# Sign of float64 weights taken by a parametric ReLU, another order of the first steps, reloads in place

## The chip, the cores and the metric

One core of one Trainium2 chip. The time is the device time of one execution in microseconds, as the median of the runs. TensorE, VectorE, ScalarE and GpSimd run in order, each on its own list; all DMAs are issued from SP's one queue.

## What is computed

Batch 4, 8 heads, 576 positions, 64 columns a head. Attention has two parts: one over q, k and v averaged in groups of 4 positions, repeated 4 times, and one over the neighbours at a distance under 4. Their sum, as 2304 rows of 512, goes through two MLPs of the same form. The weights reach the kernel as float64 words.

```python
def _moe_ref(x, w_in, w_out):
    h = x @ w_in                  # 2304 x 512 by 512 x 2048
    r = np.maximum(h, 0.0)
    g = r * r
    return (g @ w_out).astype(np.float32)

def reference(**kwargs):
    ...
    attn_out = _attn_ref(**attn_kwargs)     # out_up + out_local
    x = np.ascontiguousarray(attn_out.transpose(0, 2, 1, 3)).reshape(B * S, H * D)
    x = _moe_ref(x=x, **moe_kwargs)
    return _moe2_ref(x=x, **moe2_kwargs)
```

## The kernel before

The 2304 rows are 9 tiles of 256, the hidden width 8 blocks `p` of 256. One step (n, p) takes tile n through block p: `mm_h` (line 883) makes h from x and w_in in 24 matmuls, ScalarE makes relu and square in PSUM (lines 895, 897), and `mm_y` (line 967) adds its product with w_out, 24 matmuls in the first layer. Every operand is split in a high and a low float32r half, so that three products stand for one of full float32. The second layer, tiles n = 9 to 17, makes y by seven products of halves (`mm_y2`, line 950, 21 matmuls), for which `quarters` prepares sums of blocks of w_out.

The weights of the first layer are converted at the start by `convert1(p, kind)`, kind 0 for w_in and 1 for w_out: the float64 block is loaded into `s`; ScalarE reads the high words as float32 and scales them into a buffer `g` (line 693), and scales the low words in place (line 695); VectorE puts the sign bit of the high word into the low word's place (line 697), shifts `g` left by 3 and joins it with the low word (line 702); ScalarE copies the result to the high half (line 390 of the helper `evac`), VectorE or GpSimd subtracts for the low half (line 713). `convert2` does the same for the second layer in halves of 512 columns (lines 739, 741, 743, 747) while the first layer runs, and stores the words in DRAM; `reload` (lines 823 to 829) brings them back when the first layer is done with a block: a load into a staging buffer `ld`, a copy to the high half, a subtraction for the low half.

The attention of batch b feeds the tiles: `load_qk` (transposes, line 450, evacuation, line 390, pooling on VectorE, line 457), `pool_v`, `heads_of` (the pooled part), `values`, `group` (the local part; line 619 scales the softmax, line 623 transposes it, line 653 adds both parts to `xr`). `split_x` splits x.

The order of all engines' instructions is written out by a planner when the program is built: the class `Order` holds threads (generators) in lanes of a given width, each with a due time in tiles; it always takes the operation that can start first by its own cost figures, and at a tie the thread of the earliest due time. Conversions are due at `CP + CD * p`, loads of q and k at `t + QP`, the pooling of v at `t + VP`, the heads at `t + HP`, groups and values at their place plus `GP` and `UP`, with t = b * 576 / 256 - 2. What the planner sets is an order for each engine; on the chip an instruction waits for its operands by semaphores, and all that stands behind it on its engine waits too. Until the first step, `fill` puts dummy matmuls between the attention's (line 1121).

The first two tiles go side by side. With `LEAD = 2`, the steps by tile are 0 0 0 1 0 1 0 1 0 1 0 1 0 1 1 1; tile 1's y has a PSUM pair of its own. PSUM pairs `at0`, `at1` and `y` serve the attention until the steps take them.

Of the kernel before, what the change touches and what calls it, by code (L numbers as in the profile page):

```python
# [8 lines left out]
F32 = mybir.dt.float32  # L9
# [5 lines left out]
AF = mybir.ActivationFunctionType  # L15
# [19 lines left out]
NXR = 2  # L35
NVW, NPB, NHD = 2, 2, 2
AHEAD = 4
LEAD = 2
XO = 'PVHL'
XN = [2, 2, 2, 5]  # L40
PO = 80
# [3 lines left out]
FT = 3  # L45
KICK = {(n, 1) for n in (10, 12, 14)}
CL, GL, HL = 4, 4, 6
CP, CD, GP, UP = -0.47, 0.09, -1.99, -1.02
QP, VP, HP = -0.59, 0.34, -0.14


class Thread:
# [162 lines left out]
def attention_two_mlp_kernel(  # L215
# [154 lines left out]
    def dvp(cols):  # L370

        return "DVP", 0.065 + cols / 957.0
# [7 lines left out]
    def act(cols):  # L380
        return "ACT", 0.065 + cols / 1150.0
# [7 lines left out]
    def evac(dst, src):  # L389
        nc.scalar.activation(out=dst, in_=src, func=AF.Copy)  # L390

    def dma(nbytes, run=4096):

        return "SP", nbytes / (16e3 * run) * {256: 22.5, 1024: 88.0, 2048: 142.0, 4096: 212.0}[run]
# [271 lines left out]
    def convert1(p, kind):  # L666
        yield lambda: 0.0
        for slots, i in spare.get((p, kind), []):
            yield from slots.give_up([i])
        st = early[p, kind] if (p, kind) in early else buffer(p, kind, I64, "s")  # L670
        st = st[:, 0:1024]
        if kind == 0:
            t = st.rearrange("p (r i f) -> p r i f", r=2, i=2)
            wv = w_in1.rearrange("(s i r d) f -> s r d i f", s=2, i=2, r=2)
            for r in range(2):
                for s_ in range(2):
                    tt = yield dma(64 * 4096, 2048)
                    nc.sync.dma_start(out=t[64 * s_:64 * s_ + 64, r ^ s_], in_=wv[s_, r][:, :, p * 256:p * 256 + 256])
        else:
            for half in range(2):  # L680
                r0 = p * 256 + half * 128
                tt = yield dma(64 * 8192)
                nc.sync.dma_start(out=st[:, 512 * half:512 * half + 512], in_=w_out1[r0:r0 + 128])
        wf = st.bitcast(F32).rearrange("p (c w) -> p c w", w=2)[:, :, 1]
        wl = st.bitcast(U32).rearrange("p (c w) -> p c w", w=2)[:, :, 0]
        w32 = st.bitcast(I32).rearrange("p (c w) -> p c w", w=2)
        m = yield from f_ga.take()
        parts = [(gp, 0, 1024)] if m == 0 else [(gb[i], 512 * i, 512) for i in range(2)]


        for g, c, n in parts:
            yield act(n)
            nc.scalar.activation(out=g, in_=wf[:, c:c + n], func=AF.Copy, scale=2.0 ** -112)
        yield act(1024)
        nc.scalar.activation(out=wl, in_=wl, func=AF.Copy, scale=2.0 ** -29 - 2.0 ** -49, bias=-0.5)
        yield dvp(1024)
        nc.vector.scalar_tensor_tensor(
            out=w32[:, :, 0], in0=w32[:, :, 1], scalar=-2 ** 31, in1=w32[:, :, 0], op0=ALU.bitwise_and, op1=ALU.bitwise_or
        )
        for g, c, n in parts:  # L700
            yield dvp(n)
            nc.vector.scalar_tensor_tensor(
                out=g.bitcast(I32), in0=g.bitcast(I32), scalar=3, in1=w32[:, c:c + n, 0],
                op0=ALU.logical_shift_left, op1=ALU.bitwise_or,
            )
        hi = weight(p, kind, 0).rearrange("p k f -> p (k f)")
        for g, c, n in parts:
            yield act(n)
            evac(hi[:, c:c + n], g)
        for g, c, n in parts:  # L710
            for lo, c1, n1 in pieces(p, kind, 1, 1, c, n):
                tt = yield either(n1)
                engine().tensor_tensor(
                    out=lo, in0=g[:, c1 - c:c1 - c + n1], in1=hi[:, c1:c1 + n1].bitcast(F32), op=ALU.subtract
                )
        f_ga.put(m, tt)
        count(("w", 1, p), 2, tt)
        count(("w", 1), 2 * NP, tt)

    def convert2(p, kind, half):  # L720
        yield o.at("w", 1)
        n = yield from f_ld.take()
        if kind == 0:
            t = ld[n].rearrange("p (k f) -> p k f", k=2)
            yield dma(64 * 8192, 2048)
            nc.sync.dma_start(
                out=t, in_=w_in2.rearrange("(k p) f -> p k f", p=128)[:, 2 * half:2 * half + 2, p * 256:p * 256 + 256]
            )
        else:
            r0 = p * 256 + half * 128  # L730
            yield dma(64 * 8192)
            nc.sync.dma_start(out=ld[n], in_=w_out2[r0:r0 + 128])
        wf = ld[n].bitcast(F32).rearrange("p (c w) -> p c w", w=2)[:, :, 1]
        wl = ld[n].bitcast(U32).rearrange("p (c w) -> p c w", w=2)[:, :, 0]
        w32 = ld[n].bitcast(I32).rearrange("p (c w) -> p c w", w=2)
        m = yield from f_gb.take()
        g = gb[m]
        yield act(512)
        nc.scalar.activation(out=g, in_=wf, func=AF.Copy, scale=2.0 ** -112)
        yield act(512)  # L740
        nc.scalar.activation(out=wl, in_=wl, func=AF.Copy, scale=2.0 ** -29 - 2.0 ** -49, bias=-0.5)
        yield dvp(512)
        nc.vector.scalar_tensor_tensor(
            out=w32[:, :, 0], in0=w32[:, :, 1], scalar=-2 ** 31, in1=w32[:, :, 0], op0=ALU.bitwise_and, op1=ALU.bitwise_or
        )
        tt = yield dvp(512)
        nc.vector.scalar_tensor_tensor(
            out=g.bitcast(I32), in0=g.bitcast(I32), scalar=3, in1=w32[:, :, 0],
            op0=ALU.logical_shift_left, op1=ALU.bitwise_or,
        )  # L750
        f_ld.put(n, tt)
        tt = yield dma(128 * 2048)
        nc.sync.dma_start(out=wscr[p][kind][:, half * 512:half * 512 + 512], in_=g)
        count(("scr", p, kind), 2, tt)
        f_gb.put(m, tt)
# [23 lines left out]
                units = units[3:]  # L779
        ev["room"] = 0.0  # L780

    def quarters(p0):
        yield lambda: ev.get("room")
        for p in range(p0, NP, 2):
            n = yield from f_ld.take()
            t = ld[n].bitcast(F32).rearrange("p (m c) -> p m c", m=4)
            yield dma(128 * 4096)
# [26 lines left out]
    def reload(p, kind):  # L814
        yield o.at("scr", p, kind)
        if kind == 0:
            yield o.at("h", NT - 1, p)
        else:
            yield o.at("y", NT - 1, p)
        n = yield from f_ld.take()  # L820
        t = ld[n].bitcast(F32)
        yield dma(128 * 4096)
        nc.sync.dma_start(out=t, in_=wscr[p][kind])
        hi = weight(p, kind, 0, 2).rearrange("p k f -> p (k f)")
        yield act(1024)
        evac(hi, t)
        for lo, c, n1 in pieces(p, kind, 1, 2, 0, 1024):
            tt = yield either(n1)
            engine().tensor_tensor(out=lo, in0=t[:, c:c + n1], in1=hi[:, c:c + n1].bitcast(F32), op=ALU.subtract)
        f_ld.put(n, tt)  # L830
        count(("w", 2, p), 2, tt)


# [27 lines left out]
            f_xr.put(i, tt)  # L861
            ev["split", n] = tt

    steps = []
    for p in range(NP + LEAD):
        steps += [(0, p)] * (p < NP) + [(1, p - LEAD)] * (p >= LEAD)
    steps += [(n, p) for n in range(2, len(seq)) for p in range(NP)]

    def mm_h(i, fi):
# [104 lines left out]
                    )  # L974

    def ybs(n):
        return [pair[1][:, i] for i in range(2)] if n == 1 and LEAD < NP else yb

    def products():
        def y(i):  # L980
            n, p = steps[i]
            yield o.at("gh", i)
            if p == 0 and n > (LEAD < NP) and n < NT:
                yield o.at("left", n - 1 if n != 2 or LEAD == NP else 0)
            if seq[n][0] == 2:
                if p == 0 and n > NT:
                    yield o.at("left", n - 2)
# [20 lines left out]
        for i, (n, p) in enumerate(steps):  # L1008
# [14 lines left out]
            if i == 0:  # L1023
                o.fill = None
                yield from f_at.give_up([2])
            if LEAD < NP and (n, p) == (1, 0):
                yield from f_at.give_up([1])
            yield o.at("w", seq[n][0], p)
            if i > 1:
# [9 lines left out]
    def leave():  # L1039
        for n, (layer, t) in enumerate(seq):  # L1040
# [34 lines left out]
                    nc.sync.dma_start(out=out[t * TN + 128:(t + 1) * TN], in_=yst[:, 512:1024])  # L1075
                    return
            ev["left", n] = tt
            if n == 1 and LEAD < NP:
                f_at.back(1, tt)
            tt = yield dma(128 * 4096)  # L1080
            if layer == 1:
# [8 lines left out]

    heads, groups, vees = [], [], []
    for b in range(B):
        t = b * S / TN - 2
        heads += [(t + QP, load_qk(b, c)) for c in range(5)]
        heads += [(t + VP, pool_v(b, kh, j)) for kh in range(2) for j in range(2)]
        heads += [(t + HP, heads_of(b, hp)) for hp in range(4)]
        vees += [((b * S + GQ * i) / TN + UP, values(b, i)) for i in range(NG)]
        groups += [((b * S + GQ * i) / TN + GP, group(b, i)) for i in range(NG)]

    first_w = [(CP + CD * p, convert1(p, kind)) for p in range(NP) for kind in range(2)]  # L1100
    second_w = [(99, convert2(p, kind, half)) for p in range(NP) for kind in range(2) for half in range(2)]

    o.lane(1, [(-9, act_h())])
# [3 lines left out]
    o.lane(1, [(-5, fetch(n)) for n in range(NT, 2 * NT)])  # L1107
    o.lane(1, [(98, make_room())])
    o.lane(1, [(0, more_later())])
    o.lane(2, [(98, quarters(0)), (98, quarters(1))])  # L1110
    o.lane(2, [(-4, reload(p, kind)) for p in range(NP) for kind in range(2)])
    o.lane(CL, first_w)
    o.lane(GL, groups)
# [62 lines left out]
```

## Time and profile before

| what | value |
|---|---|
| median of the runs | 926.19 us |
| lowest run | 924.8 us |
| the profiled execution | 928.45 us |
| its span, first to last instruction | 926.6 us |
| mean granted TensorE clock | 0.989 |
| busy: TensorE, VectorE, ScalarE, GpSimd | 895.9, 533.5, 525.2, 70.4 us |

The span and the rows are of the profiled execution. Busy time is a mean over very unlike stages, and TensorE's contains the dummy matmuls of the start. A granted clock of 1.00 is 2.4 GHz, 0.50 is 1.2 GHz. Times are counted from the span's start.

### The profile page before, as it was taken

To read this page: it belongs to the slowest core of one execution; us is meant where nothing else is said; L and a number is where in the kernel's file an instruction comes from. 1 tells how busy PE (TensorE), PEld (TensorE's weight loads), DVE (VectorE), ACT (ScalarE), POOL (GpSimd) and SP (SyncE) were. 2 spreads that over 40 slices of the span, in tenths; PEclk is the share of its full clock that TensorE was granted. 3 is DMA by queue.
4 is the path that set the end of the run, shared out by engine and by line. 5 is a ranking of instruction groups with operands and counts; after the bars stand their busy time and mean duration, and the time that the engine had idled before them with its cause. 6 is when DMAs were issued, how large, how long until landed. Compare 5 with 4: busy or idle time off the path is not lost.

```text
span 926.6 us, 20891 instructions
## 1 busy us (share of the span) xinstructions
PE 895.9 (97%) x8712; PEld 860.9 (93%) x8712; DVE 533.5 (58%) x1072; ACT 525.2 (57%) x1029; POOL 70.4 (8%) x72
## 2 busy tenths in 40 slices
PE   8967999999999999999999999999999999999996
PEld 5566999999989999999999999999999999999996
DVE  5898875375685656554412466646556464545454
ACT  4787884466467566664535665455555554545443
POOL 4102210020030100000100001000000000000000
PEclk9978999999999999999999999999999999999999
DMA  9997931135255665753203441101010010100000
GB/s 173 248 247 187 229 100 36 48 109 125 52 163 170 185 196 183 238 182 102 93 1 138 137 159 48 46 1 46 2 46 24 24 47 1 47 1 24 1 24 23
DMA packets 91998, 90.48 MB, mean 98 GB/s; under 512 B 62208, under 2 KB 67840, under 8 KB 91904
## 3 DMA queue, kind: packets, MB, share of 16 engines
q1 hardware_dynamic: 91904, 89.15, 33.9%
q8 instruction: 68, 1.11, 0.5%
q14 instruction: 26, 0.21, 0.1%
HBM read 70.25 MB, written 18.87 MB: 96 GB/s over the span
## 4 chain that ended last, share of the span: by engine, by line
PE 85%; DVE 5%; DMA 4%; ACT 3%; SPq 2%; issue 1%; ACTq 0%; DVEq 0%
PE h L883 40%; PE y L967 19%; PE at L950 12%; PE y L950 4%; PE at L967 2%; DMA s<-in_moe_w_out_dram 1%; PE at L450 1%; DVE S L930 1%; DMA ld<-in_v_dram 1%; SPq L437 1%; DVE ld L1072 1%; PE at L641 1%; PE at L586 1%; PE at L516 1%; PE at L476 1%
## 5 line engine op out<-in xcount | busy, mean ns | idle before, releaser
L883 PE MATMUL h<-xH,w 128*128 128x256 f32 x2304 | 318.7, 281 | 0.0
L883 PEld LDWEIGHTS h<-xH,w 128*128 128x128 f32 x2304 | 289.0, 189 | 2.4 <-issue 1.6
L895 ACT ACTIVATE h<-h 128x512 f32<-128x512 f32 x144 | 83.9, 583 | 195.6 <-PE h L883 195.5
L967 PE MATMUL y<-g,w 128*128 128x256 f32 x1536 | 193.1, 280 | 0.2 <-ACT g L907 0.2
L967 PEld LDWEIGHTS y<-g,w 128*128 128x128 f32 x1536 | 182.2, 189 | 3.2 <-issue 1.2
L883 PE MATMUL h<-xL,w 128*128 128x256 f32 x1152 | 180.2, 279 | 0.0
L934 DVE TENSOR_TENSOR g<-h,g 128x512 fp32r<-128x512 f32 x144 | 98.6, 684 | 106.2 <-ACT g L907 105.8
L883 PEld LDWEIGHTS h<-xL,w 128*128 128x128 f32 x1152 | 154.7, 189 | 0.0
L930 DVE TENSOR_TENSOR S<-h,S 128x128 f32<-128x128 f32 x144 | 41.9, 291 | 154.8 <-ACT g L907 150.5
L913 ACT CAST SH<-S 128x512 fp32r<-128x512 f32 x72 | 44.7, 621 | 93.2 <-DVE S L930 91.0
L897 ACT ACTIVATE h<-h 128x512 f32<-128x512 f32 x144 | 84.2, 585 | 3.1
L907 ACT CAST g<-h 128x512 fp32r<-128x512 f32 x144 | 84.8, 589 | 1.5
L939 DVE TENSOR_TENSOR gSL<-S,SH 128x512 fp32r<-128x512 f32 x72 | 51.1, 709 | 9.9 <-ACT SH L913 1.5
L858 POOL TENSOR_TENSOR xL<-xr,xH 128x512 fp32r<-128x512 f32 x12 | 18.0, 1504 | 408.2 <-ACT xH L390 408.2
L950 PE MATMUL at<-w,SH 128*128 128x256 f32 x224 | 45.0, 282 | 1.4 <-ACT SH L913 1.4
L930 DVE TENSOR_TENSOR S<-S,h 128x128 f32<-128x128 f32 x144 | 41.2, 286 | 5.0
L950 PEld LDWEIGHTS at<-w,SH 128*128 128x128 f32 x224 | 34.0, 188 | 2.3 <-ACT SH L913 2.2
L950 PE MATMUL at<-w,g 128*128 128x256 f32 x240 | 34.6, 279 | 0.4 <-DVE g L934 0.4
L950 PE MATMUL at<-w,gSL 128*128 128x256 f32 x112 | 32.1, 287 | 1.9 <-DVE gSL L939 1.9
L950 PEld LDWEIGHTS at<-w,g 128*128 128x128 f32 x240 | 30.8, 188 | 0.6 <-DVE g L934 0.6
L950 PE MATMUL y<-w,g 128*128 128x256 f32 x192 | 27.6, 279 | 0.0
L457 DVE TENSOR_REDUCE qkd<-at 128x256 f32<-128x1024 f32 (+1 forms) x19 | 20.7, 1106 | 9.3 <-ACT qkT L390 9.1
(252 smaller groups left out, 1238.0 us busy)
## 6 DMA issues: line engine op xcount, KB each, us to landing
ld<-ws SPq DMA_DIRECT2D x24, 512.0 KB, 3.2
s<-in_moe_w_in_dram SPq DMA_DIRECT2D x32, 256.0 KB, 3.7
s<-in_moe_w_out_dram SPq DMA_DIRECT2D x16, 512.0 KB, 10.9
ws<-ga SPq DMA_DIRECT2D x32, 256.0 KB, 2.4
ld<-in_moe_w_in_dram SPq DMA_DIRECT2D x11, 512.0 KB
ld<-in_moe_w_out_dram SPq DMA_DIRECT2D x11, 512.0 KB, 4.7
xr<-ys SPq DMA_DIRECT2D x9, 512.0 KB, 3.7
vw<-in_v_dram SPq DMA_DIRECT2D x68, 64.0 KB, 3.0
```

The costliest lines, as they stand in the source:

```text
L457: nc.vector.tensor_reduce(out=qkd[:, :, :, 32 * c:32 * c + n // 4], in_=got.rearrange("p z m (g r) -> p z m g r", r=4), op=ALU.add, axis=AX.X,
L858: engine().tensor_tensor(out=xL[n % NXL][:, ks], in0=xr[i][:, ks], in1=xH[n % NXL][:, ks].bitcast(F32), op=ALU.subtract)
L883: nc.tensor.matmul(out=o, lhsT=wt[p, 0][:, 1084:1340][:, fs] if w is wL and kk == 0 and p in ODD else w[:, kk, fs], rhs=x[:, kk], start=(i ...
L895: nc.scalar.activation(out=h, in_=h, func=AF.Relu)
L897: nc.scalar.activation(out=h, in_=h, func=AF.Square)
L907: nc.scalar.copy(g_of(i, 0), h)
L913: nc.scalar.copy(late2["SH"], late2["S"])
L930: nc.vector.tensor_tensor(out=dst, in0=a, in1=b, op=op)
L934: nc.vector.tensor_tensor(out=g_of(i, 1), in0=h, in1=g_of(i, 0).bitcast(F32), op=ALU.subtract)
L939: nc.vector.tensor_tensor(out=late2["SL"], in0=late2["S"], in1=late2["SH"].bitcast(F32), op=ALU.subtract)
L950: nc.tensor.matmul(out=seven(n, m - 1), lhsT=lhsT, rhs=quarter(p, w, low), start=p == 0 and x == 0 and m not in (2, 3, 6), stop=p == NP - ...
L967: nc.tensor.matmul(out=yb[e // 2][:, (e % 2) * 256:(e % 2) * 256 + 256], lhsT=w[:, fi, e * 128:e * 128 + 128], rhs=g[:, fi * 256:fi * 256 ...
```

## The change

In both conversions ScalarE's first pass becomes a parametric ReLU: positive words are scaled by 2^-112 as before, negative ones by 2^-112 * 2^32. The shift by 3 brings the bit that this sets to the sign's place, and the VectorE operation that fetched the sign (lines 697 and 743) goes. The steps of tiles 0 and 1 follow the string `TURNS`: 0 0 0 1 1 0 1 0 1 1 0 0 0 1 1 1. Nine due times change, and batch 1 gets offsets of its own, `H1` and `G1`; the two kinds of one block get due times `CK` apart. `reload` loads straight into the low half's place, copies from there to the high half and subtracts in place; no staging buffer is taken, and a low half in two pieces (w_in of p = 0, 3 and 6) is loaded and copied in two. The quarter blocks are made by one thread in place of two.

```diff
-LEAD = 2
+TURNS = "0001101011000111"
...
-CP, CD, GP, UP = -0.47, 0.09, -1.99, -1.02
-QP, VP, HP = -0.59, 0.34, -0.14
+CP, CD, GP, UP = -0.848, 0.436, -1.416, -1.019
+QP, VP, HP = -0.537, 0.649, -0.76
+CK, H1, G1 = 0.154, 0.689, -0.118
...
-            nc.scalar.activation(out=g, in_=wf[:, c:c + n], func=AF.Copy, scale=2.0 ** -112)
+            nc.scalar.activation(out=g, in_=wf[:, c:c + n], func=AF.Prelu, scale=2.0 ** -112, alpha=2.0 ** 32)
         yield act(1024)
         nc.scalar.activation(out=wl, in_=wl, func=AF.Copy, scale=2.0 ** -29 - 2.0 ** -49, bias=-0.5)
-        yield dvp(1024)
-        nc.vector.scalar_tensor_tensor(
-            out=w32[:, :, 0], in0=w32[:, :, 1], scalar=-2 ** 31, in1=w32[:, :, 0], op0=ALU.bitwise_and, op1=ALU.bitwise_or
-        )
...
-        nc.scalar.activation(out=g, in_=wf, func=AF.Copy, scale=2.0 ** -112)
+        nc.scalar.activation(out=g, in_=wf, func=AF.Prelu, scale=2.0 ** -112, alpha=2.0 ** 32)
...
-        yield dvp(512)
-        nc.vector.scalar_tensor_tensor(
-            out=w32[:, :, 0], in0=w32[:, :, 1], scalar=-2 ** 31, in1=w32[:, :, 0], op0=ALU.bitwise_and, op1=ALU.bitwise_or
-        )
...
-    def quarters(p0):
+    def quarters():
         yield lambda: ev.get("room")
-        for p in range(p0, NP, 2):
+        for p in range(NP):
...
-        n = yield from f_ld.take()
-        t = ld[n].bitcast(F32)
-        yield dma(128 * 4096)
-        nc.sync.dma_start(out=t, in_=wscr[p][kind])
+
         hi = weight(p, kind, 0, 2).rearrange("p k f -> p (k f)")
-        yield act(1024)
-        evac(hi, t)
-        for lo, c, n1 in pieces(p, kind, 1, 2, 0, 1024):
+        some = pieces(p, kind, 1, 2, 0, 1024)
+        for lo, c, n1 in some:
+            yield dma(128 * 4 * n1, 4096 if n1 == 1024 else 2048)
+            nc.sync.dma_start(out=lo.bitcast(F32), in_=wscr[p][kind][:, c:c + n1])
+        for lo, c, n1 in some:
+            yield act(n1)
+            evac(hi[:, c:c + n1], lo.bitcast(F32))
+        for lo, c, n1 in some:
             tt = yield either(n1)
-            engine().tensor_tensor(out=lo, in0=t[:, c:c + n1], in1=hi[:, c:c + n1].bitcast(F32), op=ALU.subtract)
-        f_ld.put(n, tt)
+            engine().tensor_tensor(out=lo, in0=lo.bitcast(F32), in1=hi[:, c:c + n1].bitcast(F32), op=ALU.subtract)
...
-    steps = []
-    for p in range(NP + LEAD):
-        steps += [(0, p)] * (p < NP) + [(1, p - LEAD)] * (p >= LEAD)
+    steps = [(int(n), TURNS[:i].count(n)) for i, n in enumerate(TURNS)]
...
-        t = b * S / TN - 2
+        t = b * S / TN - 2 + (b == 1) * H1
...
-        vees += [((b * S + GQ * i) / TN + UP, values(b, i)) for i in range(NG)]
-        groups += [((b * S + GQ * i) / TN + GP, group(b, i)) for i in range(NG)]
...
-    first_w = [(CP + CD * p, convert1(p, kind)) for p in range(NP) for kind in range(2)]
+        vees += [((b * S + GQ * i) / TN + UP + (b == 1) * H1, values(b, i)) for i in range(NG)]
+        groups += [((b * S + GQ * i) / TN + GP + (b == 1) * G1, group(b, i)) for i in range(NG)]
+
+    first_w = [(CP + CD * p + CK * kind, convert1(p, kind)) for p in range(NP) for kind in range(2)]
...
-    o.lane(2, [(98, quarters(0)), (98, quarters(1))])
+    o.lane(1, [(98, quarters())])
```

## Rows read from the trace of the kernel before

**Rows 1.** Windows: stretch, length, busy PE, PEld, DVE, ACT, POOL, clock, DMA share, GB/s.

```profile
36.00:49.80 13.80, 11.67 (x203) 6.74 (x201) 13.41 (x24) 10.51 (x16) 0.00 (x0) 0.97 0.91 224
49.80:59.00 9.20, 2.98 (x16) 2.77 (x14) 9.13 (x16) 6.71 (x9) 0.00 (x0) 0.69 1.12 260
59.00:74.00 15.00, 14.53 (x135) 13.90 (x135) 12.43 (x18) 11.22 (x18) 0.00 (x0) 0.88 1.10 238
74.00:83.00 9.00, 2.48 (x22) 2.29 (x21) 7.56 (x10) 8.41 (x11) 0.75 (x1) 0.81 1.00 244
83.00:91.70 8.70, 8.70 (x91) 8.18 (x89) 7.41 (x7) 5.87 (x9) 4.96 (x5) 0.80 0.38 110
91.70:160.00 68.30, 68.30 (x689) 64.89 (x686) 49.67 (x81) 50.51 (x103) 8.17 (x5) 1.00 0.51 121
160.00:300.00 140.00, 139.16 (x1723) 131.37 (x1723) 86.47 (x170) 81.45 (x189) 18.81 (x15) 1.00 0.41 112
300.00:540.00 240.00, 240.00 (x2313) 238.28 (x2312) 113.62 (x199) 133.92 (x241) 11.68 (x12) 1.00 0.45 148
...
762.00:906.00 144.00, 144.00 (x1225) 144.00 (x1224) 74.14 (x186) 71.64 (x142) 3.69 (x2) 1.00 0.04 16
```

**Rows 2.** Waits between 36 and 91.7 us: who for whom, us, times, longest.

```profile
PE at L450 <- DVE qkd L457: 6.5, 1, 6.5
...
PE at L623 <- ACT w L390: 6.2, 1, 6.2
```

**Rows 3.** The chain that ended last up to 100 us: start, us, what.

```profile
29.63 12.90 DMA s<-in_moe_w_out_dram
...
53.51 5.10 DMA vw<-in_v_dram
58.61 1.20 DVE s L697
...
71.53 1.23 DVE s L697
...
77.79 1.24 DVE s L697
...
80.35 1.14 DVE s L697
...
82.67 1.97 PE at L450 x8
...
86.34 0.96 PE at L450 x8
```

**Rows 4.** Groups by line and form, whole run: busy us, mean ns, idle before.

```profile
L697 DVE SCALAR_TENSOR_TENSOR s<-s 128x1024 int32<-128x1024 int32 x16 | 19.6, 1222 | 6.6 <-ACT s L695 6.4
...
L390 ACT ACTIVATE w<-ld 128x1024 fp32r<-128x1024 f32 x16 | 17.0, 1062 | 0.4 <-DMA ld<-ws 0.4
...
L743 DVE SCALAR_TENSOR_TENSOR ld<-ld 128x512 int32<-128x512 int32 x22 | 15.1, 690 | 14.6 <-ACT ld L741 14.6
...
L693 ACT ACTIVATE gp<-s 128x1024 f32<-128x1024 f32 x8 | 9.2, 1147 | 2.5 <-DVE w L713 2.5
```

**Rows 5.** The chain that ended last, whole run: start, us, what.

```profile
500.12 2.72 PE h L883 x24
...
575.20 2.38 PE at L950 x21
...
631.24 2.83 PE h L883 x24
634.07 2.47 PE at L950 x21
```

**Rows 6.** Timeline of ScalarE: its table load, the first conversion, the last turn.

```profile
0.73 1.28 ACT L390 ACT_TABLE_LOAD   x1 [0.73 <-PEq L1160]
...
34.73 1.15 ACT L693 ACTIVATE gp<-s 128x1024 f32<-128x1024 f32 x1
...
366.43 0.68 ACT L739 ACTIVATE ga<-ld 128x512 f32<-128x512 f32 x1
```

More of the change, by code (lines that the diff above doesn't have):

```diff
@@ L976, in ybs @@
     def ybs(n):
-        return [pair[1][:, i] for i in range(2)] if n == 1 and LEAD < NP else yb
+        return [pair[1][:, i] for i in range(2)] if n == 1 else yb
     def products():
@@ L982, in y @@
             yield o.at("gh", i)
-            if p == 0 and n > (LEAD < NP) and n < NT:
-                yield o.at("left", n - 1 if n != 2 or LEAD == NP else 0)
+            if p == 0 and n > 1 and n < NT:
+                yield o.at("left", n - 1 if n != 2 else 0)
             if seq[n][0] == 2:
@@ L1025, in products @@
                 yield from f_at.give_up([2])
-            if LEAD < NP and (n, p) == (1, 0):
+            if (n, p) == (1, 0):
                 yield from f_at.give_up([1])
@@ L1077, in leave @@
             ev["left", n] = tt
-            if n == 1 and LEAD < NP:
+            if n == 1:
                 f_at.back(1, tt)
```

## The prediction

> **What bounds the kernel now.** I read the windows first, then the waits, then the chain, then single prices. The windows [rows 1] split the run in two. From 91.7 us on TensorE has no idle time that the windows can show (68.30 of 68.30 us, 240.00 of 240.00 us between 300 and 540), so work taken from VectorE or ScalarE there buys nothing by itself. Before it lies the only stretch with holes: TensorE is busy 2.98 of the 9.2 us from 49.8, 14.53 of 15, 2.48 of 9 and 8.70 of 8.7, in all 28.69 of 41.9 us, so 13.2 us are idle. The granted clock is below 1.00 in all four windows; 0.88 over 15 us and 0.80 over 8.7 us mean 3.6 and 3.5 us at 1.2 instead of 2.4 GHz, each after a hole, which costs half of that, 3.5 us. So 13.2 + 3.5 = 16.7 us is all that a better start can win once the first matmul of the MLP has been issued at 49.8.
>
> The waits name the two holes [rows 2]: 6.2 us before the transposes of line 623 (put down to ScalarE, but the softmax scaling of line 619 on VectorE feeds them) and 6.5 us before line 450, the transposes of batch 1's q and k, whose PSUM pair is freed by VectorE's pooling of line 457. In that stretch VectorE is the fullest of the feeders: 9.13 of 9.2 us, 12.43 of 15, 7.56 of 9, and 13.41 of 13.8 us just before [rows 1]. The chain [rows 3] limits this reading: up to 58.6 us it runs over DMAs and SP's queue (12.90 us for one w_out block, 5.10 us for a v block), and only from there over VectorE and ScalarE, with the sign operation of line 697 on it four times: 1.20, 1.23, 1.24 and 1.14 us. It shows the price of the low clock too: eight transposes take 1.97 us right after the second hole and 0.96 us later.
>
> **The change part by part.** *Sign operation (lines 697 and 743).* Removed: 16 instructions of 1222 ns and, of the second layer's 32, 22 at 690 ns from one form alone [rows 4]. The second kind runs between 160 and 540 us, where TensorE has 139.16 of 140 and 240.00 of 240 us: 22 x 0.69 = 15.2 us of VectorE and nothing on the path; the cover is TensorE's own work, and VectorE at 86.47 of 140 us would have to fill up before it went. Of the first kind, those after 58.6 us that stand in the chain count in full: 1.20 + 1.23 + 1.24 + 1.14 = 4.8 us. Those before it stand beside the DMA chain. Bounds: 0, or four times 1.22 = 4.9 us if VectorE at 13.41 of 13.8 us sets the start; the chain is the nearer row, so I take 0. The 16 do not win more after 91.7 us. Next late is ScalarE, which in the four windows is busy 6.71, 11.22, 8.41 and 5.87 us, 32.2 of 41.9, against VectorE's 36.5 less the 4.8 of the chain, 31.7: it becomes the fuller of the two, so I count no more than the 4.8 us for this edit.
>
> *Prelu in the place of Copy.* No instruction is added. Prelu does not run in this trace. The nearest rows are the Copy that it replaces, 1147 ns with every second word read, and an evacuation of as many columns in one piece at 1062 ns [rows 4]: 0.09 us lie between two ScalarE forms of one size, so I bound it by -0.09 and +0.09 us for each 1024 columns, some eight blocks before 91.7 us, -0.7 to +0.7 us, and take 0, as the operands keep their layout.
>
> *Order of the first 16 steps and due times.* Same steps, same matmuls, no instruction more. Tile 0's fourth step goes behind tile 1's first two, so blocks of p = 3 are wanted one step later and tile 1's x at the same fourth place. Batch 1's loads, poolings and heads get due times 0.689 tiles later (and QP, VP, HP, GP shift them again: -0.34 becomes 0.40 for its q and k), while conversions of p = 2 and 3 go from -0.29 and -0.20 to 0.02 and 0.46. So q and k of batch 1, ten DMAs on SP's one queue, fall behind more of the weights, and their transposes, evacuations (line 390) and poolings (line 457) leave the place where TensorE, in order, waited 6.5 us for them. Of that hole 1.23 + 1.24 + 1.14 = 3.6 us are counted above; 6.5 - 3.6 = 2.9 us remain, and half of the 3.5 us at the low clock behind it, 1.7 us. I take both as won. Bounds: 0, if the wait goes to the next instruction that stands too early in the order, and all of what is left, 16.7 - 4.8 = 11.9 us. The poolings and transposes themselves are not saved: they lie later, between TensorE's products.
>
> *Reloads in place.* The loads go straight into the low half, so 16 takes of a staging buffer fall away; three blocks split in 256 and 768 columns give three more DMAs, three more ScalarE and no more VectorE instructions. The new wait: the DMA may only start when TensorE has read the old low half in the last tile of the first layer; behind it on SP stand the fetch of the next x and the store of y. A block is wanted a tile later, 8 steps of twice 2.72 us, 43.5 us [rows 5], and 300 to 540 us is full of TensorE work, so 0; without that cover a wait would cost what is left of a step, some 3 us. One lane for the quarter blocks in place of two is under the same cover: 0.
>
> Sum: 4.8 + 2.9 + 1.7 = 9.4 us. The profiled execution took 928.45 us (1.85 us outside its span of 926.6), so 919.05; the median of the runs is 926.19, 2.3 us lower, and on it the forecast is 926.19 - 9.4 = 916.8, said as 917.
>
> **The rivals.** *The start is bound by transfers.* The chain up to 58.6 us speaks for it. Then the holes fill less: the four sign operations give half, 2.4 us, the order nothing: 924.
>
> *The order is better than I count.* All of 16.7 us, and the 4.9 us in front: 926.2 - 21.6 = 904.6. Against it: x of tile 1 needs all of batch 0's groups, and conversions keep their other two VectorE passes.
>
> *The pace of the matmuls.* At a granted clock of 1.00 the same 24 matmuls take 2.72 us in some stretches and 2.83 in others, and the 21 of the second layer 2.38 or 2.47 [rows 5]. No row shows why a stretch has its pace, so an order that moves TensorE's stops may move it too. If 300 to 540 us (44 pairs of 5.44 us) went to the slow pace, it would cost 44 x 0.22 = 9.7 us; if 762 to 906 (27 steps of 5.30 us [rows 1, 5]) went to the fast one, it would give 27 x 0.20 = 5.4 us. With my 9.4 that makes 926.5 or 911. A few more slow steps in the second layer, 28 at 0.20 = 5.6 us, give 932: slower than before, from the point where more than 9.4 us of pace is lost, that is 43 slow pairs.
>
> *Table loads, ending on the slow side.* One load of 1.28 us at 0.73 us serves Copy, Exp, Relu and Square for the whole run [rows 6]. If Prelu stood in another set than Exp, each turn between a conversion and a softmax would cost one. Conversions and exponentials alternate 27 times in ScalarE's order between the first conversion at 34.73 and the last turn at 366.43 [rows 6], 16 of them by 160 us. Five fall between 34 and 51 us, around the first matmul, 5 x 1.28 = 6.4 us on the path; the eleven after 91.7, 14.1 us, fall into a window in which ScalarE has only 68.3 - 50.5 = 17.8 us to spare, and I put half on the path, 7.0 us. 916.8 + 6.4 + 7.0 = 930.2, slower than before from the eighth load on the path. For this rival speaks the Trainium skill, page ScalarE: Activation LUTs, section "Table sets: the hidden batching unit": functions come in named sets, and its list of what the exp set holds does not name Prelu; against it, the same section says that cheap functions fill every set, and no run here shows which. By that page's figure of about 2.66 us for a load with its drain the same sixteen would weigh about twice as much.
>
> *The change doesn't do what it says* in one way only: the conversions' dependency is unchanged, and line 702 still waits for both ScalarE passes; if those were late anyway, removing 697 leaves its time as waiting. That is the first rival's price.
>
> **How the numbers follow.** Forecast 0.50 (911 to 922 with its own bounds); bound by transfers, 924, 0.18; better order 905, 0.08; pace faster by 5.4 us, 911, 0.09; pace slower, 926.5 to 932, 0.10; table loads 930 or more, 0.05. Two per cent, about what a measurement of this kernel can tell from no change, is 18.5 us: under 907.7 lie the better order, part of the forecast with a fast pace, 0.15 in all; over 944.7 only table loads that all reach the path, or a new hole with a slow pace, 0.04; the rest, 0.81. The range takes in the full 21.6 us at one end and the slow pace at the other: 905 to 930.
>
> **What would show it.** Right: no line 697 and 743; VectorE between 49.8 and 91.7 us down by about 9 us; no wait of more than 3 us before line 450; the first unbroken run of line 883 and 967 near 82 us in place of 91.7; one table load; Prelu near 1147 ns. Wrong: a new hole before another attention transpose, ScalarE full where VectorE was, the pace of 2.83 between 300 and 540 us, or idle TensorE around 540 us behind a late reload. The weakest step is the order: the 2.9 us are the wait's remainder in a place that may no longer exist.

## The result, and the profile after

The changed kernel took 913.93 us (913.23 to 915.1), where the kernel before took 924.8 to 930.5 beside it: ratio 0.9855 [0.9825, 0.9885]. One execution of the kernel before, the first, took 1109.7 us and is left out. A second set of runs gave 911.33 against 925.0, ratio 0.9863 [0.9843, 0.9884]. That is 12 to 14 us less, surely a gain and under two per cent; the forecast was 917, in a range from 905 to 930. The profiled execution took 915.1 us, its span 913.3, against 928.45 and 926.6.

The windows of the changed kernel, with the columns and stretches of [rows 1]:

```profile
49.80:59.00 9.20, 6.69 (x60) 5.62 (x59) 9.10 (x13) 8.79 (x13) 3.03 (x2) 0.63 1.08 247
59.00:74.00 15.00, 14.34 (x148) 13.72 (x148) 12.06 (x21) 15.00 (x24) 0.38 (x1) 1.00 1.10 207
74.00:83.00 9.00, 9.00 (x82) 9.00 (x81) 6.19 (x6) 6.75 (x9) 0.92 (x1) 1.00 1.11 250
83.00:91.70 8.70, 8.70 (x79) 8.51 (x78) 5.64 (x7) 6.75 (x10) 2.00 (x2) 1.00 0.95 249
...
300.00:540.00 240.00, 237.90 (x2217) 236.28 (x2208) 100.94 (x177) 134.82 (x243) 13.52 (x13) 0.99 0.43 142
```

TensorE is idle for 2.51 + 0.66 = 3.2 of the 41.9 us, where it was idle for 13.2, and from 59 us on its clock is full in this stretch. VectorE has 33.0 us of work there instead of 36.5; ScalarE has 37.3 instead of 32.2 and not a gap between 59 and 74. The first matmul of the MLP hardly moved, from 49.83 to 49.20 us.

The waits of TensorE in the changed kernel (who for whom, us, times, longest) answer to [rows 2]:

```profile
PE h L877 <- DVE xL L854: 2.1, 2, 1.7
PE at L944 <- ACT SH L907: 1.9, 1, 1.9
PE h L877 <- ACT xH L392: 1.7, 1, 1.7
```

The 6.5 us before the transposes of q and k (now line 452) and the 6.2 us before those of the softmax (now line 625) are both gone. The chain that ended last, up to 100 us (start, us, what), against [rows 3]:

```profile
46.04 8.26 DMA s<-in_moe_w_in_dram
54.32 5.73 DMA e<-in_v_dram
60.09 0.61 ACT h L891
60.70 1.07 ACT gp L696
...
65.28 1.04 ACT s L698
...
71.46 1.07 ACT gp L696
72.53 0.48 ACT g L901
73.06 2.99 PE y L961 x24
76.05 0.87 PE at L452 x8
76.93 4.11 PE h L877 x36
```

DMAs up to 60 us, as before; then ScalarE where VectorE's sign operations stood; from 73.06 us TensorE alone, where in the kernel before TensorE's own work begins at 82.67. The transposes take 0.87 us where they took 1.97 after the hole.

Prelu and the table, by the groups (busy us, mean ns, idle before) and by ScalarE's timeline, against [rows 4, 6]; the last line is the relu of step 3, used as a mark below:

```profile
L738 ACT ACTIVATE ga<-ld 128x512 f32<-128x512 f32 x22 | 14.9, 678 | 2.1 <-DMA ws<-ga 1.7
L696 ACT ACTIVATE gp<-s 128x1024 f32<-128x1024 f32 x9 | 10.3, 1148 | 0.0
```

```profile
0.73 1.28 ACT L392 ACT_TABLE_LOAD   x1 [0.73 <-PEq L1154]
...
79.71 0.58 ACT L889 ACTIVATE h<-h 128x512 f32<-128x512 f32 x1 [1.69 <-PE h L877]
```

One load for the whole run, and 1148 ns where Copy took 1147.

To see where time is won, each profile is read at the same places: the start of the relu of some steps (counted in the order of the steps), as the difference to the profile of before, where they stand at 94.7, 185.7, 407.2, 451.1, 535.6 and 580.4 us. The start of the first MLP matmul stands beside them.

| kernel | first h at | step 3 | 16 | 48 | 56 | 72 | 80 | median, us | ratio to before |
|---|---|---|---|---|---|---|---|---|---|
| after | 49.2 | -15.0 | -13.9 | -12.8 | -12.8 | -12.8 | -12.1 | 913.93 | 0.9855 |
| x2_sign_gone | 47.8 | -6.0 | -6.0 | -6.3 | -6.3 | -6.3 | -6.3 | 920.30 | 0.9940 |
| x1_sign_back | 52.9 | -6.8 | +1.7 | +3.3 | +3.3 | +3.3 | +2.5 | 925.16 | 0.9978 |
| x3_prelu_only | 52.8 | +21.9 | +22.5 | +17.1 | +24.2 | +24.2 | +24.1 | 951.87 | 1.0256 |
| x4_order_only | 52.6 | +7.9 | +8.3 | +4.7 | +11.1 | +11.1 | +11.1 | 936.86 | 1.0101 |
| x7_old_due | 52.6 | +18.0 | +19.4 | +13.9 | +13.9 | +13.9 | +13.0 | 939.79 | 1.0169 |
| x6_old_turns | 50.7 | -13.5 | -4.2 | -5.0 | -5.0 | -5.0 | -4.3 | 919.50 | 0.9932 |
| x5_old_reload | 48.5 | -15.7 | -14.5 | -13.5 | -6.4 | -6.4 | -6.5 | 918.81 | 0.9922 |
| x8_two_lanes | 48.2 | -15.9 | -14.7 | -13.4 | -7.4 | -7.4 | -6.6 | 917.75 | 0.9927 |
| k2_one_more | 46.4 | -15.5 | -14.4 | -13.6 | -13.6 | -13.6 | -12.9 | 911.99 | 0.9852 |
| after_again | 48.4 | -15.8 | -14.7 | -13.9 | -13.9 | -13.9 | -13.2 | 911.33 | 0.9863 |
| x9_late_reload | 49.5 | -14.7 | -13.6 | -12.8 | -12.8 | -12.8 | -15.1 | 910.05 | 0.9848 |
| x10_late_and_kick | 47.4 | -16.8 | -15.3 | -13.9 | -13.9 | -13.9 | -15.5 | 909.91 | 0.9840 |

The whole gain is there at step 3. From step 3 to step 48 some 2 us go back without a stop of TensorE over 0.3 us: before that mark stand 502 attention matmuls in place of 562, and the other 60 now stand behind it. The first matmul comes at 46.4 to 49.5 us in the seven profiles that have the same instructions up to there (after, after_again, x5, x8, x9, x10, k2), so up to 3 us of a row are the start of one execution. A row shows one execution and a median several: x6's profile took 923.93 us, 4.4 above its median. What the profiles win or lose behind step 80 is in no column; of the 4.1 us between those of after and after_again, 3 arise there, at the pace told under k2.

### The profile page after: what moved, and what is told of

It is laid out like the page before. It is cut to its first block, busy times and chain, and to the rows that moved or that the text cites. A ratio compares the mean times of both kernels' runs of the same rounds, so it can differ in the third digit from the quotient of the medians.

```text
span 913.3 us, 20806 instructions
## 1 busy us (share of the span) xinstructions
PE 894.6 (98%) x8696; PEld 859.1 (94%) x8696; DVE 496.0 (54%) x1016; ACT 524.6 (57%) x1030; POOL 72.6 (8%) x78
## 4 chain that ended last, share of the span: by engine, by line
PE 83%; DVE 5%; DMA 4%; ACT 4%; issue 1%; SPq 1%; POOL 0%; ACTq 0%; POOLq 0%
PE h L877 39%; PE y L961 18%; PE at L944 12%; PE y L944 4%; PE at L961 3%; DMA s<-in_moe_w_out_dram 2%; DVE S L924 1%; PE at L452 1%; DVE ld L1066 1%; DMA ld<-in_v_dram 1%; PE at L643 1%; DMA s<-in_moe_w_in_dram 1%; DVE xL L854 1%; PE at L588 1%; PE at L478 1%
## 5 line engine op out<-in xcount | busy, mean ns | idle before, releaser
L961 PE MATMUL y<-g,w 128*128 128x256 f32 x1536 | 191.0, 279 | 0.7 <-ACT g L901 0.6
L928 DVE TENSOR_TENSOR g<-h,g 128x512 fp32r<-128x512 f32 x144 | 98.6, 685 | 115.7 <-ACT g L901 113.5
L924 DVE TENSOR_TENSOR S<-h,S 128x128 f32<-128x128 f32 x144 | 41.9, 291 | 158.0 <-ACT g L901 152.8
L392 ACT ACTIVATE qkT<-at 128x1024 f32<-128x1024 f32 (+1 forms) x19 | 17.8, 936 | 16.9 <-PE at L452 16.7
```

The costliest lines, as they stand in the source:

```text
L924: nc.vector.tensor_tensor(out=dst, in0=a, in1=b, op=op)
L928: nc.vector.tensor_tensor(out=g_of(i, 1), in0=h, in1=g_of(i, 0).bitcast(F32), op=ALU.subtract)
L961: nc.tensor.matmul(out=yb[e // 2][:, (e % 2) * 256:(e % 2) * 256 + 256], lhsT=w[:, fi, e * 128:e * 128 + 128], rhs=g[:, fi * 256:fi * 256 ...
```

## The experiments

Theory A was the prediction's own sum: the sign operation is worth about 4.8 us through VectorE at the start, the order the rest. Theory B was that the order makes the gain and the sign operation next to nothing.

**x2_sign_gone.** The kernel before with its engine orders kept instruction for instruction; Prelu carries the sign, and the planner still sets aside VectorE's time, but the operation is not issued.

```diff
-            nc.scalar.activation(out=g, in_=wf[:, c:c + n], func=AF.Copy, scale=2.0 ** -112)
+            nc.scalar.activation(out=g, in_=wf[:, c:c + n], func=AF.Prelu, scale=2.0 ** -112, alpha=2.0 ** 32)
...
         yield dvp(1024)
-        nc.vector.scalar_tensor_tensor(
-            out=w32[:, :, 0], in0=w32[:, :, 1], scalar=-2 ** 31, in1=w32[:, :, 0], op0=ALU.bitwise_and, op1=ALU.bitwise_or
-        )
```

> The kernel before with its order of all engines kept, Prelu in the place of Copy and the sign operation left out in all 48 places (its time is still in the planner's sums, so nothing else moves). Theory A: the chain loses its four operations, 4.8 us, so 0.5% under the kernel before; the wait before the transposes of batch 1 shrinks from 6.5 to about 3 us. Theory B: less than 1.5 us gained, the wait stays above 5 us.

Measured 920.3, ratio 0.994 [0.991, 0.997]: 5.6 us less. Its waits of TensorE between 36 and 91.7 us:

```profile
PE at L623 <- ACT w L390: 6.2, 1, 6.2
PE at L450 <- DVE qkd L457: 2.3, 1, 2.3
```

The hole that VectorE made is down from 6.5 to 2.3 us; the other stays whole. Theory A's term for the sign operation holds. It is all won by step 3: from there to step 72 the row keeps its -6.0 to -6.3, so the operations of the second layer, between 160 and 540 us, are worth nothing.

**x1_sign_back.** The changed kernel's order, with Copy in place of Prelu and the sign operation put back just ahead of the shift, without a place of its own in the plan.

```diff
-            nc.scalar.activation(out=g, in_=wf[:, c:c + n], func=AF.Prelu, scale=2.0 ** -112, alpha=2.0 ** 32)
+            nc.scalar.activation(out=g, in_=wf[:, c:c + n], func=AF.Copy, scale=2.0 ** -112)
...
             yield dvp(n)
+            if c == 0:
+                nc.vector.scalar_tensor_tensor(
+                    out=w32[:, :, 0], in0=w32[:, :, 1], scalar=-2 ** 31, in1=w32[:, :, 0],
+                    op0=ALU.bitwise_and, op1=ALU.bitwise_or
+                )
```

> The changed kernel with its order of all engines kept, but with Copy in the place of Prelu and the sign operation issued again just ahead of the shift, in all 48 places. Theory A (the sign operation is on the path of the start until the first tiles run without holes): 4 to 6 us slower than the changed kernel, so 918 to 920 us, with VectorE's four or five operations of 1.22 us between 44 and 75 us showing as later products. Theory B (ScalarE and the transfers set the pace of the start, the order did the rest): within 1.5 us of the changed kernel.

Measured 925.16, ratio 0.9978 [0.995, 1.0007]: the whole gain is gone, and both theories missed. Waits of TensorE in it:

```profile
PE h L885 <- ACT xH L392: 4.5, 1, 4.5
PE h L885 <- DVE xL L862: 2.4, 2, 1.7
PE y L969 <- ACT g L909: 2.1, 2, 1.5
PE at L508 <- ACT hd L488: 2.0, 1, 2.0
```

In the new order the operation delays the first matmul too (52.9 us), then products and heads; behind the 2.0 us stop near 150 us TensorE ran at 1.2 GHz from 151.5 to 158.3. Together with x2 this is a table of two by two, in which the order includes the reloads in place and the one thread of quarter blocks: with the operation it is worth 0.7 us (925.9 to 925.2), without it 920.3 goes to 911 to 914. The parts do not add.

**x3_prelu_only and x7_old_due.** x3 is the kernel before with Prelu, planned anew without the operation. x7 is the changed kernel with the old due times: seven numbers go back, and the three new offsets are zero.

```diff
-CP, CD, GP, UP = -0.848, 0.436, -1.416, -1.019
-QP, VP, HP = -0.537, 0.649, -0.76
-CK, H1, G1 = 0.154, 0.689, -0.118
+CP, CD, GP, UP = -0.47, 0.09, -1.99, -1.02
+QP, VP, HP = -0.59, 0.34, -0.14
+CK, H1, G1 = 0.0, 0.0, 0.0
```

> The kernel before with Prelu and without the sign operation, planned anew with the old steps and due times. Theory A: as with the kept order, 5 us gained, give or take 3 for an order that comes out otherwise. Theory B: under 2 us.

> The changed kernel with the old due times and no offsets for batch 1, all else new. Theory A: the transposes of batch 1 come early again, a wait of 3 us or more before them returns, 4 to 8 us slower. Rival (the new steps or the missing sign operation are enough): within 1.5 us.

Measured 951.87 (1.0256 [1.0216, 1.0296]) and 939.79 (1.0169 [1.0136, 1.0202]): 26.0 and 14.5 us slower than before, 25.9 us slower than after in x7's case, and far from any of the numbers expected. Windows of x7:

```profile
83.00:91.70 8.70, 3.69 (x50) 2.58 (x50) 8.30 (x14) 6.68 (x17) 0.73 (x1) 0.56 1.07 252
91.70:113.00 21.30, 9.72 (x102) 8.50 (x102) 17.85 (x36) 17.55 (x31) 1.87 (x2) 0.54 0.85 221
```

and its waits of TensorE; x3 meets the same three at 2.9, 4.3 and 4.6 us:

```profile
PE at L625 <- DVE pb L621: 4.9, 1, 4.9
PE at L625 <- DVE pb L607: 4.2, 1, 4.2
PE at L579 <- ACT hd L488: 3.9, 1, 3.9
```

With the operation gone from its list, and the old due times, the planner puts attention ahead of the products up to 113 us; TensorE, in order, goes through a series of stops at half its clock. (x3 meets a stop of 3.9 us before y as well, the 7.1 us between its steps 48 and 56; x8 below has one like it.) So the new due times do not bring a gain of their own; they fit the order to the shorter list.

**x4_order_only.** The kernel before, its sign operation planned, with the new steps and due times (diff as in the change).

> The kernel before with the new steps of tiles 0 and 1 and the new due times, sign operation, old reloads and old quarter lanes kept. Theory A: the wait for the poolings is gone but VectorE stays full, so 5 to 8 us gained, 920 to 923. Theory B: nearly all of the change's 13 us, 914 to 917.

Measured 936.86, ratio 1.0101 [1.007, 1.0132]. TensorE's timeline in it:

```profile
83.38 3.04 PE L452 MATMUL at<-ident,e 128*128 128x128 f32 x13 [6.35 <-DVE qkd L459]
```

The hole that the new order was to remove is there again, as long as before, and 7.9 us are lost by step 3. Another stop (3.6 us before y, behind ScalarE's copies of line 1047, near 414 us) takes 6.4 more; it is like that of x8 below, and x4 too has two threads of quarter blocks, so these 6.4 us cannot be put down to the steps and due times alone. This and x7 tell the same from both sides: steps, due times and list of operations make one order.

**x6_old_turns.** The changed kernel with the steps of the kernel before.

```diff
-TURNS = "0001101011000111"
+TURNS = "0001010101010111"
```

> The changed kernel with the old order of the first 16 steps (0 0 0 1 0 1 ...), all else new. Theory A (steps and due times share the gain): 2 to 5 us slower than the changed kernel, with TensorE waiting for blocks of p = 3 around 75 us. Rival (the due times do it all): within 1.5 us.

Measured 919.5, ratio 0.9932 [0.991, 0.9955]: 5.6 us more than after's 913.93. The size is near theory A, the place is not: around 75 us TensorE waits 0.6 us at most. Up to step 6 x6 keeps 1.5 us behind after; then comes one stop in TensorE's timeline, before transposes of the attention's heads, with the clock at 1.2 GHz from 110.9 to 117.7 us:

```profile
111.44 1.17 PE L508 MATMUL at<-ident,hd 72*72 72x72 f32 x8 [2.91 <-DVE pb L607]
```

**x5_old_reload and x8_two_lanes.** x5 is the changed kernel with the old reload and two threads of quarter blocks; x8 has only the two threads.

```diff
-    def quarters():
+    def quarters(p0):
...
-        for p in range(NP):
+        for p in range(p0, NP, 2):
...
-    o.lane(1, [(98, quarters())])
+    o.lane(2, [(98, quarters(0)), (98, quarters(1))])
```

> The changed kernel with the old reload through a staging buffer and the two quarter lanes. Theory A: reloads in place are worth nothing, 912 to 916 us. Rival: the stop of 2.15 us at 533 us and the low clock after it come from the reloads in place, so the old reload wins back 1 to 3 us there.

> The changed kernel with its reloads in place, but the quarter blocks made by two threads side by side again. With the old reload and two lanes a stop of 4.1 us came at 396 us, where ScalarE had eight quarter copies ahead of the two copies that free y's PSUM pair. Theory C (the two lanes make that stop, the place of the reload has no part in it): the stop is there again, with the low clock behind it 5 to 7 us, and the stop at 533 us stays: 917 to 921 us. Rival (the staging buffer that the old reload took makes it): no stop near 396 us, 912 to 916 us.

Measured 918.81 (0.9922 [0.9897, 0.9947]) and 917.75 (0.9927 [0.9903, 0.995]); in the latter's session after took 911.33, 6.4 less. The start is after's; 6 us go at one place, as theory C had it for x8. x8, timeline of TensorE, of ScalarE and of SP:

```profile
395.95 0.62 PE L877 MATMUL h<-xL,w 128*128 128x256 f32 x4
400.43 4.33 PE L961 MATMUL y<-g,w 128*128 128x256 f32 x24 [3.86 <-ACT ld L1041]
```

```profile
395.60 0.72 ACT L392 ACTIVATE q_qkT<-ld 128x256 fp32r<-128x256 f32 x2
...
398.69 0.42 ACT L392 ACTIVATE q_qkT<-ld 128x256 fp32r<-128x256 f32 x1
399.00 0.58 ACT L1041 COPY ld<-y 128x512 f32<-128x512 f32 x1
399.47 0.43 ACT L392 ACTIVATE q_qkT<-ld 128x256 fp32r<-128x256 f32 x1
399.79 0.59 ACT L1041 COPY ld<-y 128x512 f32<-128x512 f32 x1
```

```profile
376.83 0.88 SPq L783 DMA_DIRECT2D ld<-ws  x2
```

and after's SP and ScalarE in the same place:

```profile
377.38 0.38 SPq L783 DMA_DIRECT2D ld<-ws  x1
```

```profile
391.68 1.07 ACT L1041 COPY ld<-y 128x512 f32<-128x512 f32 x2 [3.09 <-PE y L961]
```

The products of y wait for ScalarE to empty y's PSUM pair (line 1041), and ScalarE has copies of quarter blocks, and the relu, square and cast of the steps that follow, ahead of that in its list. That two threads bring the stop and one does not is shown, as x8 changes nothing else. Why they do is read from the program and the traces: line 1041 copies y into a staging buffer `ld`, of which two are left at this time. Two threads load both (x8's two loads at 376.83 us), so that the copies of y find a place in the order only when one is given back; with one thread the second buffer is free, and the copies come right behind y's products. No run with a third buffer tests this. x3, x4 and x5 have two threads and such a stop; the kernel before and x2 have two threads and no such stop, so it takes an unlucky order as well. The two threads are also why x5 missed its 912 to 916 us.

x5 and x8 differ by 1.1 us with intervals that overlap, so the reload in place by itself moves the time little. From step 72 to 80 x5 keeps its lead over the kernel before and x8 loses 0.8 us. Both have the next stop; with the old reload it is shorter, and no low clock follows it (x5):

```profile
540.77 0.50 PE L944 MATMUL at<-w,SH 128*128 128x256 f32 x2 [1.08 <-ACT SH L907]
```

The kernel before has this stop too, 1.08 us at 547.19.

**x9_late_reload, x10_late_and_kick and after_again.** In the changed kernel that stop stands at 533 us and is longer (the 1.9 us at line 944 above; the expectations count 2.15, and 4.1 for x8's, from the start of the last matmul before the stop). VectorE's timeline there, then ScalarE's:

```profile
532.45 0.29 DVE L924 TENSOR_TENSOR S<-S,h 128x128 f32<-128x128 f32 x1 [0.79 <-ACT g L901]
532.66 1.22 DVE L826 TENSOR_TENSOR w<-w 128x1024 fp32r<-128x1024 f32 x1
533.79 0.28 DVE L924 TENSOR_TENSOR S<-S,h 128x128 f32<-128x128 f32 x1
534.11 0.29 DVE L924 TENSOR_TENSOR S<-h,S 128x128 f32<-128x128 f32 x1
```

```profile
530.88 1.07 ACT L392 ACTIVATE w<-w 128x1024 fp32r<-128x1024 f32 x1
531.84 0.58 ACT L901 CAST g<-h 128x512 fp32r<-128x512 f32 x1
534.49 0.62 ACT L907 CAST SH<-S 128x512 fp32r<-128x512 f32 x1 [2.07 <-DVE S L924]
```

A reload's subtraction (line 826, 1.22 us) stands between the sums of which ScalarE makes SH for the products. A reload's copy on ScalarE (line 392, 1.07 us) stands ahead of the cast for which VectorE waits 0.79 us. x9 moves both, so it can show that the reloads make the stop, but not which engine's share does. x9 lets the two reloads of the last block come later, after the h of the second layer's third block; x10 adds one dummy matmul (below); after_again is the changed kernel beside them.

```diff
             yield o.at("y", NT - 1, p)
+        if p == NP - 1:
+            yield o.at("h", NT, 2)
```

> The changed kernel in which the two reloads of the last block wait until step (9, 2) has its h; they are wanted five steps later. If the stop at 533 us (2.15 and 0.5 us, then 3.4 us at the low clock) comes from VectorE's two subtractions of these reloads, 1.22 us each, among the small sums S, it shrinks to under 1 us and the clock stays at 2.4 GHz: 2 to 4 us under the changed kernel. If it comes from the copies of y and x on ScalarE, it stays.

> The late reloads and the short matmul ahead of step (16, 4) together. The fastest of all if the stop at 533 us is cured, 908 to 911 us; the short matmul alone gave nothing that could be told from the changed kernel, so I expect the same as with the late reloads, within 2 us.

> The changed kernel itself once more, on the chip of these three, as what they are compared with: 912 to 916 us. If the pace of the matmuls in the second layer changes from run to run with the program unchanged, its slow stretches lie elsewhere in this profile than between 579 and 655 and after 831 us.

Measured 910.05, 909.91 and 911.33 (ratios [0.9826, 0.9871], [0.9811, 0.987], [0.9843, 0.9884]). One window of each, first after_again, then x9:

```profile
520.00:545.00 25.00, 22.91 (x185) 22.50 (x184) 14.79 (x30) 14.21 (x27) 2.41 (x1) 0.93 0.37 126
```

```profile
520.00:545.00 25.00, 24.49 (x211) 24.00 (x211) 17.10 (x31) 17.03 (x32) 2.40 (x1) 1.00 0.38 127
```

The stop and the low clock behind it are gone, and with them 3.0 us between steps 72 and 80 (from -12.8 to -15.1, where after_again goes from -13.9 to -13.2; 2.3 in x10). The expected 2 to 4 us are not to be seen in the medians: they keep 1.3 us, less than their intervals can part. These two are the fastest kernels seen here, about 15 us under the kernel before.

**k2_one_more.** The second layer has three dummy matmuls (`KICK`), each ahead of a step's first product. This kernel has a fourth; the question was whether they set the pace of [rows 5].

```diff
-KICK = {(n, 1) for n in (10, 12, 14)}
+KICK = {(10, 1), (12, 1), (14, 1), (16, 4)}
```

> The changed kernel with one more short bf16 matmul ahead of step (16, 4), where the matmuls run 117.8 ns apart in place of 113.5 until the end; nothing else. If a short matmul can shift a stretch from the slow to the fast pace, the last 60 us get 3.7% shorter, 2.2 us; if the pace is set by something else, no change beyond 0.5 us.

Measured 911.99, ratio 0.9852 [0.9833, 0.9871]: not to be told from after. Its second layer ran at the fast pace throughout, but also far ahead of the added matmul, and after_again, without it, did the same. The chain of after and that of after_again in the same place (start, us, what):

```profile
592.65 2.83 PE h L877 x24
...
661.49 2.72 PE h L877 x24
```

```profile
591.08 2.72 PE h L877 x24
```

One program, two paces: in one profile of the changed kernel the matmuls from 580 to 655 and from 832 to 905 us start 117.8 ns apart, in the other 113.5 ns, at a granted clock of 1.00. The dummies do not explain it: x10, which has the fourth one too, ran at the slow pace, 2.83 us for 24 matmuls, from 703 to 733 us.

## Why the prediction was right, and where it was not

**What bounds the kernel.** Right. All that the change won was won at the start. VectorE's busy time fell by 37.5 us in all (533.5 to 496.0), yet between steps 48 and 72 after keeps its -12.8 unchanged.

**Sign operation, 4.8 us.** Right: 5.6 by x2's median, 2.8 to 8.3 by its interval. The 0 for the part before the first matmul cannot be told from the spread of the start. What the text did not have is that this worth depends on the order: in the new one it is 11 to 14 us (x1).

**Prelu as Copy, 0.** Right: Prelu takes 1148 ns where Copy took 1147, and 678 where it took 677.

**Order, 4.6 us.** This is the term that was mis-sized. By the medians both parts together gave 12.3 us (926.19 to 913.93; 13.7 in the second set), so beside the 5.6 the order gave 7 to 8. The prediction counted the rest of the wait before line 450 and half of the low clock behind it; the other hole, 6.2 us before line 623, it left standing. It stays in x2 and is gone in after, with both parts. Which of the steps and due times closes it, no run separates. As an independent term the order was also wrong in kind: it is worth 0.7 us with the operation (x1), and with the operation in the plan as well it is 7.9 us slower by step 3 and 11 in all, 6.4 of them at the stop near 414 us (x4). So it is partly luck that two terms which do not add came within 3 us of the measured time. The text's own doubt, that the wait's place may no longer exist, was the right one.

**Reload and quarter blocks, 0 under cover of TensorE's work.** Near zero in sum, from step 72 to 80 after gives back 0.7 us, but for another reason than the one given. The cover did not hold: two threads of quarter blocks would have cost 6 us at 396 us (x8), and the two reloads of the last block cost the stop at 533, 3.0 us of x9's profile, of which the reload in place is some 0.9 (x8 beside x5). A window full of TensorE work says that nothing is late in this order, not that an instruction put elsewhere would not be.

**ScalarE as the next bound.** Right: it is busy 15.00 of 15 us, and the chain runs over it from 60 to 73 us.

**The signs.** Of those for right, line 697 and the long wait before line 450 are gone, there is one table load, Prelu has Copy's price, and TensorE runs without a stop from 73.06 us to past 160, earlier than from 82. VectorE's work between 49.8 and 91.7 us fell by 3.5 us only, not 9. Two of those for wrong came in part, although the forecast held: ScalarE is full where VectorE was, and TensorE stops for 1.9 us at 533 us behind a reload.

**The rivals.** The chain runs over transfers up to 60 us, as the first rival said, but its 924 was too high, since the holes behind the first matmul closed all the same. That transfers set the first matmul itself is not shown: in after it ends a wait of 1.7 us for ScalarE's xH, and with the sign operation put back it comes 3.7 us later (x1). The better order's 904.6 wanted every hole closed and 4.9 us won ahead of the first matmul; after keeps 3.2 us of idle time, 6.8 us of the 9.2 from 49.8 pass at 1.2 GHz, and the first matmul hardly moved. The pace did differ, but from run to run. The fear of table loads did not come true: there is one load. Of the two statements that the prediction quoted from the Trainium skill (ScalarE: Activation LUTs, "Table sets: the hidden batching unit"), the list without Prelu spoke for reloads; the other, that cheap functions fill every set, is the one that this trace agrees with, at least for the set in use, where one load serves Prelu and Exp. The Trainium skill's list is shortened with dots there, so it left Prelu open.

## What to carry to other kernels

Where a planner writes the order, an operation taken out changes the order as well: measure it once with the old order kept instruction for instruction and once planned anew, before a gain or a loss is put down to the operation (here -5.6 and +26 us). A hole that starts the low clock costs more than its length, so look for the next hole that an order leaves or makes, not only the one to be removed. On an engine that runs in order, ask what stands ahead of the instruction that frees a buffer, and what that instruction itself needs: with two threads of copies in place of one, the copies that empty y's PSUM pair came late enough to stop TensorE for 3.9 us in the middle of a stretch without any idle time.

## What the runs showed of the hardware

- Two paces of the same matmuls at a granted clock of 1.00, 113.5 and 117.8 ns from start to start, each kept for tens of microseconds, and differing between two executions of one program. What chooses is open.
- The same stop costs a different time at the low clock: the stop of 3.86 us near 396 us came with 1.2 GHz from 399.4 to 406.3 us in x5 and from 401.9 to 405.3 in x8. The stop of 1.9 us at 533 was followed by 3.4 us of it.
- Prelu with a second slope as large as 2^32 ran at Copy's price (1148 ns against 1147 for 128x1024) beside Exp, Copy, Relu and Square with one table load.
